# Output projections with the vector stationary and the weight rows streaming, 256 columns in each quarter of the PE array

## The chip, the cores and the metric

One core of a Trainium2 chip runs the whole program. The metric is the device time of one execution in microseconds (us); lower is better. Runs of one kernel mostly agree within about 0.15% here. The profile is of one execution; its span is about 1.8 us shorter than the device time of that execution. One profiled execution can lie away from the median of its kernel: the profile of before is of an execution of 394.29 us.

## The reference, cut to what matters

One token passes through two branches: attention over a cache of 65,536 keys (32 query heads, 4 key/value heads), and a gated MLP. A sigmoid gate mixes their outputs. The change touches only the two last matrix products, `o @ wo` and `(z1 * g) @ w_out`.

```python
def _A_ref(x, k_cache, v_cache, wq, wo):              # x 1x1x1024, caches 1x4x65536x128
    q = (x @ wq)                                       # wq 1024x4096, 32 heads of 128
    # ... softmax over 65536 keys, o: 1 x 4096
    return o @ wo                                      # wo 4096x1024
def _B_ref(x, w_in, w_sp, b_sp, w_out):
    # ... z1, g from x @ w_in: 1 x 1792 each
    return (z1 * g) @ w_out                            # w_out 1792x1024
return g * a + (1 - g) * b                             # 1 x 1 x 1024
```

Everything is bf16 with one row, so nearly all of the work is reading: 4 x 65,536 x 128 elements of K, as many of V, and about 28 MB of weights, 162 MB of loads on the page.

## The kernel before: what the change and the argument touch

Large loads go through one pool of five buffers of 32 KB a partition, all issued by SyncE in program order. The order at the end is: the last four tiles of V, `w_out` (14 chunks of 128 rows, 256 KB each), then `wo` (32 chunks), in seven pieces.

```python
WO_SPLIT = ((8, 8), (6, 4, 3, 2, 1))     # chunks of wo in each load; one buffer for each inner tuple
Q = 32                                   # columns of one quarter of the array
W = 64

def load(src, shape, name):
    t = kv.tile([P, CT * P], BF16, name=name, tag="kv")
    # [cut: a view of t in the shape asked for]
    nc.sync.dma_start(out=v, in_=src)
    return v
```

The query projection, which one experiment changes, holds a 128x128 block of weights stationary and streams one column of x, 256 times:

```python
q_ps = psm.tile([P, H], FP32, name="q_ps", tag="m")
for c in range(KC):
    w = wq_t[c // KH]
    for h in range(H):
        nc.tensor.matmul(
            q_ps[:, h:h + 1], lhsT=w[:, c % KH, h * DH:(h + 1) * DH], rhs=xT[:, c:c + 1],
            start=(c == 0 and h == 0), stop=(c == KC - 1), skip_group_check=True)
```

The output projections: eight blocks of 128x128 for a chunk, each made of every eighth column, so that partition p of the result holds eight neighbouring outputs. The vector is repeated 64 times as the moving operand.

```python
out_ps = pss.tile([P, NJ, W], FP32, name="out_ps", tag="spt")          # NJ = 8

def project(w, n, vec, c0, first=False, last=False):
    w = w.rearrange("p c (m j) -> p c j m", j=NJ)
    for c in range(n):
        for j in range(NJ):
            nc.tensor.matmul(
                out_ps[:, j, :], lhsT=w[:, c, j, :],
                rhs=vec[:, c0 + c:c0 + c + 1].to_broadcast([P, W]),
                start=(first and c == 0 and j == 0), stop=(last and c == n - 1),
                skip_group_check=True)

project(load(B_w_out.rearrange("(p c) n -> p c n", c=FC), (FC, D), "wout_t"), FC, uT, 0, first=True)
# [cut: two buffers t]
    for n in split:
        nc.sync.dma_start(out=t[:, c0 - b:c0 - b + n, :], in_=wo_view[:, c0:c0 + n, :])
        project(t[:, c0 - b:c0 - b + n, :], n, oa, c0, last=(c0 + n == OC))
        c0 += n
out_sb = const.tile([P, NJ], BF16, name="out_sb")
nc.vector.tensor_copy(out=out_sb[:], in_=out_ps[:, :, 0])
nc.sync.dma_start(out=out.rearrange("o t (p j) -> (o t p) j", j=NJ), in_=out_sb[:])
```

The value matmuls already use the streaming form: 32 stationary columns, 512 moving columns, in each of the four quarters (`o_ps[t * Q:(t + 1) * Q, :]`). In the trace of before, four of them start every 0.43 us at a granted clock of 0.50 and every 0.21 us at 1.00. They give the price of the new form.

## Time and profile before

394.06 us, median of 3 runs (393.97 to 394.17).

| | before |
|---|---|
| span of the profile | 392.5 us |
| bytes of loads, share of 16 DMA engines | 162 MB, 96.6% |
| TensorE busy | 76% |
| last matmul of the output projections ends | 389.94 us |
| cast, 128 x 8 | 0.17 us |
| output store issued, span ends | 390.16, 392.5 us |

The page of the profile before, its queues and the groups of the output projections. A queue's line gives packets, MB and the share of 16 engines' time; a group's line gives busy time, mean ns of one, and the idle time before it with what ended it:

```profile
q1 hardware_dynamic: 6480, 162.01, 96.6%
q8 instruction: 43, 0.70, 0.7%
...
L430 PE MATMUL out_ps<-oa,wo_t 128*128 128x64 bf16 x256 | 15.7, 229 | 0.6 <-DMA wo_t<-in_A_wo_dram 0.6
L430 PEld LDWEIGHTS <-wo_t 128*128 128x128 bf16 x256 | 15.6, 171 | 0.7 <-DMA wo_t<-in_A_wo_dram 0.7
...
L430 PE MATMUL out_ps<-uT,wout_t 128*128 128x64 bf16 x112 | 6.9, 235 | 3.2 <-DMA wout_t<-in_B_w_out_dram 3.2
```

DMA is the bound of the whole kernel: its queue of loads takes 96.6% of the time of the 16 engines. The projections cost 22.6 us of TensorE, and while they work on `wo` they wait 0.6 us in all.

The end of the chain of waits before, in order of time: start, duration, what.

```profile
336.97 41.19 DMA wo_t<-in_A_wo_dram
378.20 11.74 PE out_ps L430 x192
```

At 378.16 the second piece of `wo` lands, and from there 192 matmuls run without a gap to 389.94, at 61 ns each. The timeline shows the last load of `wo`, one chunk, issued by SyncE at 358.33, and the page gives 29.7 us from its issue to its landing: 388.03. So TensorE ends only 1.9 us after the last byte, and this is the most that a faster projection can give at the end.

The table by windows of the profile before: for each stretch, busy time (and instructions, those cut by an edge counted on both sides) of PE and PEld, then DVE, ACT and POOL, the granted clock, the DMA share and GB/s.

```profile
378.00:380.00 2.00, 1.80 (x30) 1.80 (x31) 0.00 (x0) 0.00 (x0) 0.00 (x0) 0.57 0.64 259
380.00:382.00 2.00, 2.00 (x37) 2.00 (x36) 0.00 (x0) 0.00 (x0) 0.00 (x0) 0.58 0.55 223
382.00:384.00 2.00, 2.00 (x37) 2.00 (x36) 0.00 (x0) 0.00 (x0) 0.00 (x0) 1.00 0.50 206
384.00:386.00 2.00, 2.00 (x37) 2.00 (x36) 0.00 (x0) 0.00 (x0) 0.00 (x0) 1.00 0.48 185
386.00:388.00 2.00, 2.00 (x37) 2.00 (x36) 0.00 (x0) 0.00 (x0) 0.00 (x0) 1.00 0.10 39
```

After 380 the DMA share is about 0.5 (0.55 to 0.48 up to 386): about half of the DMA engines have nothing left to do, while the other half needs until 386 to 388. And the pairs go at the same pace at clock 0.58 and at 1.00 (37 in 2 us), while the matmuls of the values, with 512 moving columns, take twice as long at half the clock (four in 0.43 us at 0.50, in 0.21 us at 1.00). So I take it that the moving columns do not set the 61 ns.

### The profile page before, as it was taken

The page shows a single profiled execution, that of the slowest core. Times are in us where ns is not written, and L with a number is a line of the kernel's source. Part 1 is how long each engine was busy: PE and PEld are TensorE (multiplying, and loading weights), DVE is VectorE, ACT ScalarE, POOL GpSimd, SP SyncE. Part 2 cuts the span into 40 slices and gives each one's busy share as a digit, 9 for nine tenths or more (in the row PEclk, how much of TensorE's full clock was granted, in tenths as well). Part 3 has the DMA queues.
Part 4 walks back from the last instruction along what each step waited for, and adds up shares of the span by engine and source line. Part 5 has one row for each costly group of instructions (what it writes and reads, how often), then busy time and mean ns, then how long its engine had stood idle before and what let it go on. Part 6 is the DMA issues. An engine that isn't in the chain of part 4 may idle for free.

```text
span 392.5 us, 11905 instructions
## 1 busy us (share of the span) xinstructions
PE 299.9 (76%) x5539; PEld 255.0 (65%) x5539; DVE 160.0 (41%) x316; ACT 122.2 (31%) x139; POOL 1.0 (0%) x9
## 2 busy tenths in 40 slices
PE   0774379887889985979884969689949797544697
PEld 0764379887888865857774858468738683311697
DVE  3011047574685541538551526367514357201100
ACT  1000036543594431424631423237404243100000
POOL 1000000000000000000000000000000000000000
PEclk9999999999999996999996989989978898955889
DMA  8999999999999999999999999999999999999971
GB/s 331 435 429 441 426 424 432 432 427 422 424 440 427 426 422 431 424 432 429 426 427 431 429 436 428 426 426 432 432 427 429 429 427 427 429 431 428 412 328 73
DMA packets 6566, 162.78 MB, mean 415 GB/s; under 512 B 884, under 2 KB 884, under 8 KB 1268
## 3 DMA queue, kind: packets, MB, share of 16 engines
q1 hardware_dynamic: 6480, 162.01, 96.6%
q8 instruction: 43, 0.70, 0.7%
q14 instruction: 7, 0.06, 0.0%
q10 hardware_dynamic: 36, 0.00, 0.0%
HBM read 162.01 MB, written 0.00 MB: 413 GB/s over the span
## 4 chain that ended last, share of the span: by engine, by line
DMA 50%; PE 42%; DVE 3%; issue 2%; ACT 1%; SPq 1%; DVEq 0%; ACTq 0%
DMA kn<-in_A_k_cache_dram 39%; PE tps L329 22%; DMA wo_t<-in_A_wo_dram 10%; PE spt L308 10%; PE o_ps L354 5%; PE out_ps L430 3%; DVE ktt L334 1%; DVE scT L291 1%; PE om_ps L372 1%; PE s_ps L362 1%; ACT scT L314 1%; ACT ktt L332 1%; SPq L85 0%; DVE o_sb L369 0%; PE nb_ps L286 0%
## 5 line engine op out<-in xcount | busy, mean ns | idle before, releaser
L329 PE MATMUL tps<-ident_b,kn 128*128 128x128 bf16 x2048 | 164.7, 226 | 37.3 <-DMA kn<-in_A_k_cache_dram 35.7
L329 PEld LDWEIGHTS <-kn 128*128 128x128 bf16 x2048 | 124.5, 101 | 62.8 <-DMA kn<-in_A_k_cache_dram 39.3
L334 DVE COPY ktt<-tps 128x1024 bf16<-128x1024 bf16 x171 | 116.4, 689 | 113.4 <-PE tps L329 112.6
L332 ACT COPY ktt<-tps 128x1024 bf16<-128x1024 bf16 x85 | 86.0, 1012 | 163.8 <-PE tps L329 163.8
L308 PE MATMUL spt<-qT,ktt 128*128 128x64 bf16 (+7 forms) x2048 | 104.0, 194 | 6.8 <-issue 6.7
L308 PEld LDWEIGHTS <-ktt 128*128 128x128 bf16 x2048 | 87.0, 100 | 8.4 <-issue 8.1
L354 PE MATMUL o_ps<-vt,scT 128*32 128x512 bf16 x512 | 51.9, 432 | 14.9 <-DMA vt<-in_A_v_cache_dram 14.9
L354 PEld LDWEIGHTS <-scT 128*32 128x32 bf16 x512 | 15.3, 100 | 26.7 <-issue 21.0
L314 ACT CAST scT<-spt 128x512 bf16<-128x512 f32 x32 | 18.8, 588 | 16.1 <-PE spt L308 16.1
L316 DVE TENSOR_TENSOR mxr<-scT,mxr 128x512 bf16<-128x512 bf16 x24 | 10.2, 426 | 20.3 <-ACT scT L314 18.9
L295 ACT ACTIVATE scT<-scT 128x1024 bf16<-128x1024 bf16 x16 | 16.4, 1059 | 4.9 <-DVE scT L291 4.9
L430 PE MATMUL out_ps<-oa,wo_t 128*128 128x64 bf16 x256 | 15.7, 229 | 0.6 <-DMA wo_t<-in_A_wo_dram 0.6
L430 PEld LDWEIGHTS <-wo_t 128*128 128x128 bf16 x256 | 15.6, 171 | 0.7 <-DMA wo_t<-in_A_wo_dram 0.7
L193 PE MATMUL z_ps<-xT,win_t 128*128 128x18 bf16 x224 | 13.7, 211 | 1.8 <-DMA win_t<-in_B_w_in_dram 1.3
L193 PEld LDWEIGHTS <-win_t 128*128 128x128 bf16 x224 | 13.7, 158 | 1.8 <-DMA win_t<-in_B_w_in_dram 1.4
L362 PE MATMUL s_ps<-scT,ones_b 128*32 128x512 bf16 x32 | 13.4, 418 | 0.0
L369 DVE COPY o_sb<-o_ps 128x512 f32<-128x512 f32 x4 | 2.7, 684 | 26.0 <-PE o_ps L354 26.0
L245 PE MATMUL q_ps<-xT,wq_t 128*128 128x1 bf16 x256 | 7.1, 165 | 7.6 <-DMA wq_t<-in_A_wq_dram 7.6
L245 PEld LDWEIGHTS <-wq_t 128*128 128x128 bf16 x256 | 7.0, 104 | 7.8 <-DMA wq_t<-in_A_wq_dram 7.8
L291 DVE TENSOR_TENSOR scT<-scT,negm 128x1024 bf16<-128x1024 bf16 x16 | 10.7, 683 | 0.2
L449 DVE CAST out_sb<-out_ps 128x8 bf16<-128x8 f32 x1 | 0.2, 167 | 25.1 <-PE out_ps L430 25.1
L430 PE MATMUL out_ps<-uT,wout_t 128*128 128x64 bf16 x112 | 6.9, 235 | 3.2 <-DMA wout_t<-in_B_w_out_dram 3.2
(87 smaller groups left out, 57.0 us busy)
## 6 DMA issues: line engine op xcount, KB each, us to landing
kn<-in_A_k_cache_dram SPq DMA_DIRECT2D x16, 4096.0 KB, 30.2
vt<-in_A_v_cache_dram SPq DMA_DIRECT2D x16, 4096.0 KB, 32.3
wq_t<-in_A_wq_dram SPq DMA_DIRECT2D x2, 4096.0 KB, 34.7
win_t<-in_B_w_in_dram SPq DMA_DIRECT2D x2, 3584.0 KB, 15.3
wo_t<-in_A_wo_dram SPq DMA_DIRECT2D x2, 2048.0 KB, 35.1
wout_t<-in_B_w_out_dram SPq DMA_DIRECT2D x1, 3584.0 KB
wo_t<-in_A_wo_dram SPq DMA_DIRECT2D x1, 1536.0 KB
wo_t<-in_A_wo_dram SPq DMA_DIRECT2D x1, 1024.0 KB
```

The source lines that it names most:

```text
L193: nc.tensor.matmul(z_ps[:, hf * FC + f, :], lhsT=w[:, hf, f, :], rhs=xT[:, i * KH + c:i * KH + c + 1].to_broadcast([P, zw]), start=(i == 0 ...
L245: nc.tensor.matmul(q_ps[:, h:h + 1], lhsT=w[:, c % KH, h * DH:(h + 1) * DH], rhs=xT[:, c:c + 1], start=(c == 0 and h == 0), stop=(c == KC ...
L291: nc.vector.tensor_tensor(out=blk, in0=blk, in1=negm[:].unsqueeze(1).to_broadcast([P, CT, REP]), op=ALU.add)
L295: nc.scalar.activation(out=blk, in_=blk, func=ACT.Exp, scale=SCALE)
L308: nc.tensor.matmul(spt[g][:, o:o + n], lhsT=ktt[:, j * P:(j + 1) * P], rhs=qT[:, g * REP:g * REP + n], start=True, stop=True, skip_group_c ...
L314: nc.scalar.copy(out=blk, in_=spt[g][:].rearrange("p (c h) -> p c h", h=REP))
L329: nc.tensor.transpose(tps[:, i * P:(i + 1) * P], kn[:, u * TG + i, :], ident_b[:])
L332: nc.scalar.copy(out=ktt[:], in_=tps[:])
L334: nc.vector.tensor_copy(out=ktt[:], in_=tps[:])
L354: nc.tensor.matmul(o_ps[g][t * Q:(t + 1) * Q, :], lhsT=scT[g][:, cg:cg + VC, :].rearrange("p c h -> p (c h)"), rhs=vt[:, lo:lo + VC, :].re ...
L362: nc.tensor.matmul(s_ps[g][gs, :], lhsT=ones_b[:, :Q], rhs=scT[g][:, cg:cg + CPS, :].rearrange("p c h -> p (c h)"), start=(cg == 0), stop= ...
L430: nc.tensor.matmul(out_ps[:, j, :], lhsT=w[:, c, j, :], rhs=vec[:, c0 + c:c0 + c + 1].to_broadcast([P, W]), start=(first and c == 0 and j ...
```

## The change

The intent: hold the vector stationary (one column repeated over 32 columns of the array) and stream the weight rows, 256 columns in each quarter. A chunk then takes four matmuls that should overlap as those of the values do in the trace of before (at clock 0.50 one takes up to 0.63 us, and four start every 0.43 us), each with a load of 32 stationary columns, in place of eight loads of 128 columns with eight matmuls. The result lies on four rows of 256. The split of `wo` changes too.

```diff
-WO_SPLIT = ((8, 8), (6, 4, 3, 2, 1))
+WO_SPLIT = ((16,), (8, 4, 2, 1, 1))
-    out_ps = pss.tile([P, NJ, W], FP32, name="out_ps", tag="spt")
+    NQ = P // Q
+    NO = D // NQ
+    out_ps = pss.tile([P, NO], FP32, name="out_ps", tag="spt")
     def project(w, n, vec, c0, first=False, last=False):
-        w = w.rearrange("p c (m j) -> p c j m", j=NJ)
         for c in range(n):
-            for j in range(NJ):
+            for t in range(NQ):
                 nc.tensor.matmul(
-                    out_ps[:, j, :], lhsT=w[:, c, j, :],
-                    rhs=vec[:, c0 + c:c0 + c + 1].to_broadcast([P, W]),
-                    start=(first and c == 0 and j == 0), stop=(last and c == n - 1),
+                    out_ps[t * Q:(t + 1) * Q, :],
+                    lhsT=vec[:, c0 + c:c0 + c + 1].to_broadcast([P, Q]),
+                    rhs=w[:, c, t * NO:(t + 1) * NO],
+                    start=(first and c == 0), stop=(last and c == n - 1),
                     skip_group_check=True)
-    out_sb = const.tile([P, NJ], BF16, name="out_sb")
-    nc.vector.tensor_copy(out=out_sb[:], in_=out_ps[:, :, 0])
-    nc.sync.dma_start(out=out.rearrange("o t (p j) -> (o t p) j", j=NJ), in_=out_sb[:])
+    out_sb = const.tile([P, NO], BF16, name="out_sb")
+    nc.vector.tensor_copy(out=out_sb[:], in_=out_ps[:])
+    nc.sync.dma_start(out=out.rearrange("o t (q n) -> (o t q) n", n=NO), in_=out_sb[::Q, :])
```

More of the change, by code (lines that the diff above doesn't have):

```diff
@@ L56 @@
     OC = HD // P
-    NJ = D // P
     QD = P // H
```

## The prediction

> **What bounds the kernel.** The load of the caches and weights. The page counts 162 MB on one queue, 96.6% of the span of 16 DMA engines; TensorE is busy 76%. Only the tail is open. The chain of waits ends with 41.2 us of DMA on wo_t, then 11.74 us of 192 matmuls on out_ps, unbroken from 378.20 to 389.94, then the cast (0.17 us), the output DMA (issued 390.16) and the end of the span at 392.5.
>
> **What sets those 11.74 us.** 192 LDWEIGHTS/MATMUL pairs at 61 ns, eight per 128-row chunk: 0.49 us a chunk. The last load (one chunk, 256 KB) is issued at 358.33 and lands 29.7 us later (DMA issues of the page), at 388.0. So TensorE ends only 1.9 us after the last byte. The table by windows shows why so late: after 378 the DMA share is about 0.5: half of the engines finish 8 to 10 us before the rest. The instruction queue moved 0.70 MB in 43 packets[...], and in the packet records each of these takes about 1.07 us; I read the late half as the engines that also carry them[...].
>
> **The change.** Removes 368 pairs of 128x128 weights and 64 columns; adds 184 of 128x32 weights and 256 columns, four quarters at a time. Price from the trace: the 128x512 matmuls of o_ps, which use the same quarters, go four in about 0.43 us where the granted clock is 0.50 and four in 0.21 us at 1.00; weight loads hidden. Half the columns: 0.21 us a chunk at the slow clock, 0.11 at the fast one[...]. TensorE work of the projections falls from 22.6 us to 5-10 us. But nearly all of it goes into waiting: a chunk's load costs 0.6 us, so TensorE will now wait for every piece of wo. Idle before these matmuls: 0.6 us before, about 8 to 15 us after.
>
> Bytes, buffers and order stay; wo has 6 loads, not 7. TensorE has 368 rows less, so one or two of the last instruction packets are not fetched; the one that fell at 371.8 should now come near 379.5, still on a late engine, so I leave the last landing at 387.8-388.1.
>
> **The critical path after.** Last landing 388.0; last chunk about 0.5 us with its latency (estimate from 0.376-0.634 us for one 512-column matmul): 388.5. Cast of 128x256: between 0.167 us (8 columns) and 0.684 us (512, o_sb), about 0.42: 388.95.[...] Sum: -1.9 +0.5 +0.25 -0.1 = **-1.25 us**, so 392.8 us (-0.3%). Range (8 in 10) 391.7 to 393.8. Chances: faster by over 2% 0.01, within 2% 0.98, slower 0.01.
>
> **What shows the steps right.** Out_ps matmuls busy under 11 us; the chain of waits ends in a DMA wait for wo_t, with only 4 to 8 out_ps matmuls after it; last wo_t landing at 387.5-388.3; cast 0.35-0.45 us; all before 366 us unchanged.
>
> **What would make it wrong.** If the matmuls of four quarters do not overlap at 256 columns (over 0.6 us a chunk), TensorE ends as late as before and the time is 394-396. If the missing instruction packets free the late engines, the last landing is 1.5 us earlier and the time about 391.3.[...] If the new split delays the landing, the gain vanishes.

One cut passage stood for a term of the sum: -1.9 +0.5 +0.25 -0.1 came to -1.25 us, and the -0.1 was for the output store, of whose new shape nothing had been measured; the terms that are left come to -1.15 us, or 392.9 us. The "one or two" instruction packets are an estimate from the page of before: 11,078 instructions of TensorE (5539 matmuls and 5539 weight loads) and 43 packets of the instruction queue are 258 to a packet, so 368 fewer are 1.4 packets. That the late half carries these packets, and that fewer rows would move one of them to 379.5, were estimates.

## The result, and the profile after

The changed kernel takes 392.88 us (392.74 to 393.31, 4 runs), against 394.09 us of before (393.97 to 394.17, 4 runs). The ratio is 0.9971, 95% interval 0.9954 to 0.9989: faster by 0.3%, which counts as the same at a threshold of 2%. Ratios here and below are the mean time of one kernel's runs over that of the other's of the same rounds, so not quite the ratio of the medians that are quoted.

The same lines of the page, after:

```profile
q1 hardware_dynamic: 6200, 162.01, 96.9%
q8 instruction: 42, 0.69, 0.7%
...
L430 PE MATMUL out_ps<-wo_t,oa 128*32 128x256 bf16 x128 | 7.5, 399 | 10.4 <-DMA wo_t<-in_A_wo_dram 10.4
...
L430 PEld LDWEIGHTS <-oa 128*32 128x32 bf16 x128 | 5.3, 135 | 12.8 <-issue 12.0
...
L450 DVE CAST out_sb<-out_ps 128x256 bf16<-128x256 f32 x1 | 0.4, 424 | 22.6 <-PE out_ps L430 22.6
```

The busy time on `wo` halves, 15.7 to 7.5 us, and what is saved comes back as waiting: idle before these matmuls grows from 0.6 to 10.4 us.

The end of the chain of waits after is a load; TensorE no longer has a piece in it that is worth listing:

```profile
348.63 39.01 DMA wo_t<-in_A_wo_dram
```

The timeline after, from the first piece of `wo` (start, duration, engine, line, operation, and the idle time before it). Each piece is worked off before the next one lands:

```profile
377.84 3.60 PE L430 MATMUL out_ps<-wo_t,oa 128*32 128x256 bf16 x64 [7.77 <-DMA wo_t<-in_A_wo_dram]
...
382.70 1.90 PE L430 MATMUL out_ps<-wo_t,oa 128*32 128x256 bf16 x32 [1.25 <-DMA wo_t<-in_A_wo_dram]
...
387.68 0.29 PE L430 MATMUL out_ps<-wo_t,oa 128*32 128x256 bf16 x4 [0.33 <-DMA wo_t<-in_A_wo_dram]
...
388.02 0.42 DVE L450 CAST out_sb<-out_ps 128x256 bf16<-128x256 f32 x1 [22.64 <-PE out_ps L430]
388.47 0.66 SPq L451 DMA_DIRECT2D out_dram<-out_sb  x1
```

Sixteen chunks took 3.60 us, 0.225 us a chunk, where the old form needed 0.49. Two windows of the table after:

```profile
378.00:380.00 2.00, 2.00 (x44) 1.69 (x40) 0.00 (x0) 0.00 (x0) 0.00 (x0) 0.50 0.61 258
...
384.00:386.00 2.00, 1.45 (x28) 0.90 (x21) 0.00 (x0) 0.00 (x0) 0.00 (x0) 0.50 0.44 173
```

The granted clock is 0.50 in these two windows (and 1.00 for the last three pieces, from 386.4). As each piece is worked off before the next one lands, the slow clock costs nothing here. The DMA engines are as uneven as before. The difference of the two profiles, term by term:

| term | before | after | difference, us |
|---|---|---|---|
| last landing of `wo` (completion records) | 388.06 | 387.64 | -0.42 |
| from there to the end of TensorE | 1.88 | 0.33 | -1.55 |
| cast, with the wait for it | 0.19 | 0.47 | +0.28 |
| from its end to the end of the span | 2.37 | 2.52 | +0.15 |
| span | 392.50 | 390.96 | -1.54 |

The completion records of the last piece of `wo` (sorted, us from the start of the span) show who ends last. Each load leaves 16 of them, as many as the page counts DMA engines; I read each as one engine's. The records do not name the engines.

```
before      378.31 378.34 378.55 378.87 378.96 378.96 379.69 | 382.48 | 385.89 386.00 386.25 386.30 386.35 386.39 387.85 388.06
after       377.99 378.32 378.35 378.71 378.76 378.80 379.74 | 382.32 | 385.90 385.99 386.15 386.20 386.23 386.26 386.44 387.64
```

By this reading seven engines are early, one lies between and eight are late; of these eight, two stand out by 1.5 us before, and one by 1.2 us after. The packet records give the last instruction packets (16 KB, about 1.1 us each): they start at 371.84, 379.17 and 385.79 before, and at 370.92 and 386.38 after. So before, two such packets start over 6 us before the first late engine ends (371.84 and 379.17 against 385.89), and two late engines stand out; after, one packet (370.92) and one engine. The difference of 0.42 us in the last landing is not all of that packet: over the four profiles with 42 packets (after, and experiments 1, 5 and 8) the last landing lies between 387.47 and 388.05, over the four with 43 packets (before, and experiments 2 to 4) between 387.85 and 388.07.

### The profile page after: what moved, and what is told of

Its sections match the earlier page's. It is cut to its first block, busy times and chain, and to the rows that moved or that the text cites. A ratio compares the mean times of both kernels' runs of the same rounds, so it can differ in the third digit from the quotient of the medians.

```text
span 391.0 us, 11536 instructions
## 1 busy us (share of the span) xinstructions
PE 289.8 (74%) x5355; PEld 240.1 (61%) x5355; DVE 160.2 (41%) x316; ACT 122.2 (31%) x139; POOL 1.0 (0%) x9
## 4 chain that ended last, share of the span: by engine, by line
DMA 55%; PE 39%; issue 2%; DVE 2%; ACT 1%; SPq 0%; DVEq 0%; ACTq 0%
DMA kn<-in_A_k_cache_dram 38%; PE tps L328 23%; PE spt L307 10%; DMA wo_t<-in_A_wo_dram 10%; DMA vt<-in_A_v_cache_dram 6%; PE o_ps L353 5%; DVE ktt L333 1%; ACT ktt L331 1%; PE s_ps L361 0%; PE om_ps L371 0%; SPq L84 0%; ACT scT L313 0%; DVE scT L290 0%; PE nb_ps L285 0%; PE mxT L277 0%
## 5 line engine op out<-in xcount | busy, mean ns | idle before, releaser
L353 PE MATMUL o_ps<-vt,scT 128*32 128x512 bf16 x512 | 54.2, 449 | 16.2 <-DMA vt<-in_A_v_cache_dram 15.4
L430 PE MATMUL out_ps<-wo_t,oa 128*32 128x256 bf16 x128 | 7.5, 399 | 10.4 <-DMA wo_t<-in_A_wo_dram 10.4
L192 PE MATMUL z_ps<-xT,win_t 128*128 128x18 bf16 x224 | 13.7, 208 | 1.6 <-DMA win_t<-in_B_w_in_dram 1.1
L192 PEld LDWEIGHTS <-win_t 128*128 128x128 bf16 x224 | 13.7, 158 | 1.6 <-DMA win_t<-in_B_w_in_dram 1.2
L430 PEld LDWEIGHTS <-oa 128*32 128x32 bf16 x128 | 5.3, 135 | 12.8 <-issue 12.0
L371 PE MATMUL om_ps<-o_sb,pick 128*32 128x128 f32 x32 | 5.0, 310 | 3.2 <-DVE o_sb L368 3.2
```

Source lines behind the costliest of these rows:

```text
L192: nc.tensor.matmul(z_ps[:, hf * FC + f, :], lhsT=w[:, hf, f, :], rhs=xT[:, i * KH + c:i * KH + c + 1].to_broadcast([P, zw]), start=(i == 0 ...
L353: nc.tensor.matmul(o_ps[g][t * Q:(t + 1) * Q, :], lhsT=scT[g][:, cg:cg + VC, :].rearrange("p c h -> p (c h)"), rhs=vt[:, lo:lo + VC, :].re ...
L430: nc.tensor.matmul(out_ps[t * Q:(t + 1) * Q, :], lhsT=vec[:, c0 + c:c0 + c + 1].to_broadcast([P, Q]), rhs=w[:, c, t * NO:(t + 1) * NO], st ...
```

## The experiments

Runs of the kernel before that shared the chips gave medians of 393.88 to 394.18 us.

### 1. The new form with the old split

```diff
-WO_SPLIT = ((16,), (8, 4, 2, 1, 1))
+WO_SPLIT = ((8, 8), (6, 4, 3, 2, 1))        # on the changed kernel
```

> The changed projection with the split of wo of before (8, 8, 6, 4, 3, 2, 1). Theory A (the end is set by the landing of the last piece of wo plus a fixed tail of about 0.33 us of TensorE, 0.42 us of cast and the output): the last landing is the same within 0.4 us, so the time is that of the changed kernel, 392.9 us, within 0.4. Rival B (the new split brings the gain, not the form of the matmuls): 394.0 us, as before.

Measured: 393.04 us (ratio to before 0.9977, 0.9964 to 0.9989), the last landing at 387.59 and the last matmul before 388.08. The gain is that of the whole change. The split gives nothing by itself in this form.

### 2. The old form with the new split

```diff
-WO_SPLIT = ((8, 8), (6, 4, 3, 2, 1))
+WO_SPLIT = ((16,), (8, 4, 2, 1, 1))         # on the kernel before
```

> The old projection with the new split (16, then 8, 4, 2, 1, 1). Theory A: TensorE can start on wo only when the 16-chunk piece lands, near 377.8 us, and then has 32 chunks of 0.49 us to do, so it ends near 393.5 us in place of 389.9: 397 to 398 us. Rival B (the split brings the gain): 392.9 us.

Measured: 397.87 us (1.0096, 1.0081 to 1.0112). The timeline shows 256 matmuls in one run from 377.99 to 393.56, as theory A had it:

```profile
377.99 15.57 PE L430 MATMUL out_ps<-oa,wo_t 128*128 128x64 bf16 x256 [4.14 <-DMA wo_t<-in_A_wo_dram]
```

A split that is harmless for a fast consumer costs 3.9 us with a slow one.

### 3. The old form with eleven pieces

```diff
-WO_SPLIT = ((8, 8), (6, 4, 3, 2, 1))
+WO_SPLIT = ((4, 4, 4, 4), (4, 4, 3, 2, 1, 1, 1))   # on the kernel before
```

> The old projection (128x128 weights, 64 columns, 0.49 us a chunk) with wo in eleven pieces (4, 4, 4, 4, 4, 4, 3, 2, 1, 1, 1). Theory A: a chunk's load takes about 0.62 us, longer than its 0.49 us of TensorE, so with fine pieces TensorE keeps up and ends 0.6 to 0.8 us after the last landing (1.9 us before); with the short cast (0.17 us) and the old output, 392.6 to 393.1 us: the same as the changed kernel, without the change. Rival C (the swap of operands itself is needed): 393.8 us or more.

Measured: 393.67 us (0.9993, 0.998 to 1.0005). Theory A missed here. The end of this kernel's chain of waits tells why:

```profile
331.39 35.62 DMA wout_t<-in_B_w_out_dram
367.06 22.30 PE out_ps L430 x368
```

TensorE never waits for `wo` at all: 368 pairs follow each other from the landing of `w_out`. I had priced the 32 chunks of `wo` alone (0.49 us of TensorE against 0.62 us of load), but when `w_out` lands, its 14 chunks are a backlog of 6.9 us. From that moment TensorE has 46 chunks to do, 22.3 us, while the loads still need 21.0 us (367.06 to the last landing of this run at 388.07). At 61 ns a pair the old form is bound by its throughput by about 1.3 us, whatever the split; fine pieces only recover the 0.56 us of idle time of before. The time lies between the two expectations, 0.13 us under the rival's, and is not clear of before. What the trace shows is that the projection itself has to become cheaper; that it takes the swap of operands, as the rival had it, experiment 4 does not bear out.

### 4. The old form on contiguous weights (wrong order of the result, on purpose)

```diff
-        w = w.rearrange("p c (m j) -> p c j m", j=NJ)
+        w = w.rearrange("p c (j m) -> p c j m", j=NJ)   # on the kernel of experiment 3
```

> Wrong order of the result on purpose: the old projection with eleven pieces of wo, as in the run with the fine split, but each 128x128 block of weights is 128 neighbouring columns, not every eighth. Theory I (the pair costs 61 ns because the weights are read with a step of eight elements): the pair falls to 50 to 55 ns (the score matmuls, also 64 columns on contiguous weights, take 104.0/2048 = 51 ns), the 46 chunks need about 19.5 us and TensorE waits for wo at last: it ends 0.5 to 0.9 us after the last landing, 392.9 to 393.3 us. Rival J (64 moving columns set the 61 ns): the pair stays at 61 ns, 393.7 us as with the fine split.

Measured: 393.13 us (0.9977, 0.9963 to 0.9991); TensorE ends 0.5 us after the last landing of 387.88. The groups of `wo` on the page, first of experiment 3:

```profile
L430 PE MATMUL out_ps<-oa,wo_t 128*128 128x64 bf16 x256 | 15.5, 224 | 0.0
L430 PEld LDWEIGHTS <-wo_t 128*128 128x128 bf16 x256 | 15.5, 171 | 0.0
```

and then of this run:

```profile
L430 PE MATMUL out_ps<-oa,wo_t 128*128 128x64 bf16 x256 | 12.5, 220 | 4.2 <-DMA wo_t<-in_A_wo_dram 4.2
L430 PEld LDWEIGHTS <-wo_t 128*128 128x128 bf16 x256 | 11.5, 116 | 5.1 <-DMA wo_t<-in_A_wo_dram 4.8
```

One weight load falls from 171 to 116 ns, and TensorE waits for loads again. The first 64 pairs on `wo` take 2.33 us, 36 ns each, at the full clock; at clock 0.50 32 pairs take 1.89 us, 59 ns. So the old form took 61 ns a pair because its stationary blocks were read with a step of eight elements. With contiguous blocks the pair follows the clock (36 ns at 1.00, 59 at 0.50); whether the weight load or the moving columns set its pace then, no run separates. The page of the kernel before agrees: the projection from `w_in` reads its blocks with a step of 14 elements and moves only 18 columns, and its pairs also take 61 ns (13.7 us for 224), at the full clock.

```profile
L193 PE MATMUL z_ps<-xT,win_t 128*128 128x18 bf16 x224 | 13.7, 211 | 1.8 <-DMA win_t<-in_B_w_in_dram 1.3
```

The swap of operands removes that strided weight load. Contiguous blocks would have removed most of the excess too, but then the outputs lie one by one over the partitions, and ordering them costs something that this run did not pay.

### 5. The new form with the small output (wrong result)

```diff
-    out_sb = const.tile([P, NO], BF16, name="out_sb")
-    nc.vector.tensor_copy(out=out_sb[:], in_=out_ps[:])
-    nc.sync.dma_start(out=out.rearrange("o t (q n) -> (o t q) n", n=NO), in_=out_sb[::Q, :])
+    out_sb = const.tile([P, D // P], BF16, name="out_sb")
+    nc.vector.tensor_copy(out=out_sb[:], in_=out_ps[:, :D // P])
+    nc.sync.dma_start(out=out.rearrange("o t (p j) -> (o t p) j", j=D // P), in_=out_sb[:])
```

> Wrong result on purpose: the changed kernel, but the end casts only 8 columns of 128 rows and stores 128 rows of 16 bytes, as before. Theory D (the 4-row output costs twice: 0.26 us in the cast and 0.2 to 0.3 us between issue and end, 2.53 against 2.34 us in the two traces): 392.3 to 392.5 us, 0.45 us under the changed kernel, and the span ends 2.3 us after the issue of the store. Rival (the store costs the same in both shapes): 0.26 us under the changed kernel and 2.5 us from issue to end.

Measured: 392.49 us, 0.4 us under the changed kernel. In its profile the cast takes 0.17 us and the store is issued at 388.74, with the span ending at 390.98: 2.24 us, where the changed kernel takes 2.49 (388.47 to 390.96). Its last landing happened to be at 388.05 in the profiled run, which was its slowest, 392.77; from the last landing to the end of the span it takes 2.93 us, against 3.32 in the changed kernel, again 0.4 us less. The cast gives 0.26 us of this. The store of four rows of 512 bytes costs SyncE 0.66 us of issue, against 0.35 us for 128 rows of 16 bytes: this alone is more than the store's share of the difference.

### 6. Fewer TensorE rows at the start (wrong result)

```diff
-    for c in range(KC):
+    for c in (0, 4, KC - 1):                  # q projection of the changed kernel
```

> Wrong result on purpose: the changed kernel with 160 of the 256 weight-load and matmul pairs of the q projection left out (near the start, where TensorE waits for loads anyway), 324 TensorE rows fewer. Theory E (one engine carries one instruction packet more than the other late ones, the packet at 370.9 us, and so lands the last piece 1.2 us after the third-last engine, 387.64 against 386.44 us): that packet is no longer fetched before the end, the last landing is near 386.4 us and the time 1.0 to 1.3 us under the changed kernel: 391.6 to 391.9 us. Rival (the instruction packets have nothing to do with which engine lands last): 392.9 us, last landing 387.6 us.

Measured: 391.52 us (0.9937, 0.9922 to 0.9953), 1.4 us under the changed kernel. The comparison with the reference passed it all the same, though its q is wrong. The page counts 160 matmuls and 160 weight loads fewer, so 320 rows (instructions of TensorE) and not 324 as expected. The instruction queue has 40 packets in place of 42. The last landing is 386.31, and no engine stands out any more, while the first engines end no earlier than before (378.27, and 377.99 in the changed kernel). Work that was left out between 32 and 45 us, some 345 us before the end, where TensorE waits for loads anyway (7.6 us before these matmuls), moved the last landing by 1.3 us.

### 7. A correct version of it: the streamed q

In the diff, `...` stands for `start`, `stop` and `skip_group_check`.

```diff
-    q_ps = psm.tile([P, H], FP32, name="q_ps", tag="m")
+    q_ps = [pss.tile([P, 512], FP32, name="q_ps", tag="spt") for _ in range(2)]
     for c in range(KC):
-        w = wq_t[c // KH]
-        for h in range(H):
-            nc.tensor.matmul(q_ps[:, h:h + 1], lhsT=w[:, c % KH, h * DH:(h + 1) * DH], rhs=xT[:, c:c + 1], ...)
+        for s in range(2):
+            for t in range(P // Q):
+                lo = t * (HD * Q // P) + s * 512
+                nc.tensor.matmul(q_ps[s][t * Q:(t + 1) * Q, :],
+                                 lhsT=xT[:, c:c + 1].to_broadcast([P, Q]),
+                                 rhs=wq_t[c // KH][:, c % KH, lo:lo + 512], ...)
+    q_sb = const.tile([P, REP * P], BF16, name="q_sb")
+    nc.vector.tensor_copy(out=q_sb[:, :512], in_=q_ps[0][:])
+    nc.scalar.copy(out=q_sb[:, 512:], in_=q_ps[1][:])
+    qt_ps = pst.tile([P, TG * P], BF16, name="tps")
+    for j in range(REP):
+        nc.tensor.transpose(qt_ps[:, j * P:(j + 1) * P], q_sb[:, j * P:(j + 1) * P], ident_b[:])
-    nc.vector.tensor_copy(out=qT[:, :H], in_=q_ps[:])
+    nc.vector.tensor_copy(out=qT[:, :H].rearrange("p (t j) -> p j t", j=REP),
+                          in_=qt_ps[:].rearrange("p (j t r) -> p j t r", j=REP, r=Q)[:, :, :, 0])
```

> A correct version with fewer TensorE rows: the changed kernel, with the q projection also streamed (x stationary, 512 columns of wq in each quarter, then eight 128x128 transposes): 72 pairs in place of 256, 368 rows fewer. Theory E (the number of TensorE rows sets how many instruction packets the late engines carry, and the first packet of a new round of eight costs the last landing 1.2 us): last landing near 386.4 us and the same time as with 160 pairs left out, 391.3 to 391.8 us. Rival (that run gained from the work left out at the start): 392.7 us or more.

Measured: 391.50 us (391.41 to 391.65), ratio to before 0.9937 (0.9924 to 0.9949), and correct. It beats both kernels. The projection of q itself is no faster: 7.1 us of busy time before, 7.2 us now, with 1.0 us of transposes. What it buys is rows. Over the pages, rows and packets fall together: 11,078 instructions of TensorE and 43 packets before, 10,710 and 42 in the changed kernel, 10,390 and 40 in experiment 6, 10,342 and 40 here, so 255 to 260 to a packet. Its queue of instructions, and the last lines of its timeline:

```profile
q8 instruction: 40, 0.66, 0.7%
```

```profile
386.30 0.40 PE L440 MATMUL out_ps<-wo_t,oa 128*32 128x256 bf16 x4 [0.23 <-DMA wo_t<-in_A_wo_dram]
386.75 0.42 DVE L460 CAST out_sb<-out_ps 128x256 bf16<-128x256 f32 x1 [21.32 <-PE out_ps L440]
387.20 0.65 SPq L461 DMA_DIRECT2D out_dram<-out_sb  x1
```

The completion records of its last piece:

```
streamed q  378.29 378.34 378.45 378.59 378.74 379.11 379.89 | 382.15 | 386.01 386.02 386.05 386.05 386.10 386.16 386.19 386.25
```

All eight late engines now end within 0.25 us. Forty packets would be five for each of eight engines; in the changed kernel, where the 41st starts at 370.92, well before the late engines end, one engine ends 1.2 us after the others. That the number of rows moves the last landing is shown by two runs with different edits (386.31 in experiment 6 and 386.25 here, against 387.64). That the packets go round eight engines in turn is a reading, as the records name no engines, but the completion records of earlier loads bear it out. Four of the large loads, with the packets that had started by their last completion: of the late half, as many engines end over 1 us after the others as packets are left over from whole rounds of eight, before and after the change alike:

| packets so far | 10 | 22 | 31 | 40 |
|---|---|---|---|---|
| first completion of the load, before, us | 97.55 | 184.92 | 262.60 | 350.01 |
| engines that stand out, before | 2 | 6 | 7 | 0 |
| engines that stand out, after | 2 | 6 | 7 | 0 |
| late half behind the early one, before, us | 2.1 | 4.3 | 6.0 | 7.7 |

The last line is the mean of the eight latest completions less the fourth. It is 0.2 us in the first load, before any of these packets, grows with them, and stays between 7.4 and 7.7 us from 340 to 371 us, while no packet starts between 342.72 and 371.84. So these records put the lag of the late half down to the instruction packets, at about 1.5 us for each round of eight (7.7 us after five). A packet itself takes about 1.1 us; what the rest is, and why one engine lies between the halves, stays open.

### 8. One megabyte of `wo` for half of the engines: written as 8 x 16 partitions

```diff
-WO_SPLIT = ((16,), (8, 4, 2, 1, 1))
+WO_SPLIT = ((12, 4), (8, 4, 2, 1, 1))
+            if c0 == 12:
+                nc.sync.dma_start(out=t[:, c0 - b:c0 - b + n, :],
+                    in_=A_wo.rearrange("(a e c) n -> a e c n", a=8, c=OC)[:, :, c0:c0 + n, :])
+            # [cut: else, the load as before]
```

If the early engines could carry more of the last bytes, the late ones would end earlier. Theory F is that eight engines carry this megabyte and that they are the early half; then each late one has 64 KB less to move, about 2.4 us (an estimate: four packets of 16 KB, each 614 ns in the median of the packet records of before). Rival G is that they are the late half, which then have as much more; rival H that all sixteen carry it, or some of each half. That this edit would bring it onto eight engines was the author's supposition; no run here shows it, and the reasons given are cut, here and in experiments 9 and 11.

> The changed kernel with the 16-chunk piece of wo split into 12 chunks and 4 chunks, and the 4 chunks (1 MB) loaded with the DRAM side written as 8 x 16 partitions.[...] Theory F[...]: the last landing moves from 387.6 to about 385.2 us and the time falls to 390.3 to 391 us. Rival G[...]: the last landing moves to about 390 us, time 395.3 us. Rival H[...]: within 0.4 us of 392.9, or in between.

Measured: 392.96 us, against 392.88 of the changed kernel, and the piece left 16 completion records like any other, so rival H. Nothing is learned about which engines are early.

### 9 and 10. The same megabyte as sixteen loads of 8 partitions

Experiment 9 is on the changed kernel, 10 on the one with the streamed q.

```diff
+            if c0 == 12:
+                for i in range(0, P, 8):
+                    nc.scalar.dma_start(out=t[i:i + 8, c0 - b:c0 - b + n, :],
+                                        in_=wo_view[i:i + 8, c0:c0 + n, :])
+            # [cut: WO_SPLIT as in 8; else, the load as before]
```

> The changed kernel with 4 of the first 16 chunks of wo (1 MB) loaded as 16 loads of 8 partitions each, issued by ScalarE.[...] Theory F[...]: last landing near 385.2 us, time 390.3 to 391 us. Rival G[...]: last landing near 390 us, time 395.3 us. Rival H (mixed): in between, or as the changed kernel. Whatever the engines, if the sixteen loads come too late, TensorE's wait for them shows in the timeline before chunk 12.

> Both together. If theories E and F hold, the gains add, up to the engine that lies between the two halves (382.3 us in the changed kernel): last landing near 384.5 us, time 389.3 to 390.2 us. If G holds: 394 us.

Measured: 407.30 and 407.05 us. The timeline of the first one shows SyncE issuing its last four pieces of `wo` over 37.5 us from 353.34, and ScalarE twelve of its loads over 42 us from 353.14, and TensorE waiting 12.04 us before chunk 12. In the trace the loads share eight completion semaphores. ScalarE's load at 373.33, for one, follows the landing, at 373.3, of the load that used its semaphore before, and SyncE waits 49.9 us in all for landings of `wo`. The loads came too late, so neither F nor G is tested.

### 11 and 12. Fewer loads of odd width

On the kernel with the streamed q, the 16-chunk piece in five loads, all from SyncE, and then, as a control, in two. Theories F to H are those of experiment 8, for the four loads of 8 partitions. Theory K is that the load of 96 partitions slows the packets even without loads of 8.

```diff
+            cuts = [0, P] if c0 else [0, 96, 104, 112, 120, P]      # 11: four_small_pieces
+            cuts = [0, P] if c0 else [0, 96, P]                     # 12: two_part_piece
+            for lo, hi in zip(cuts, cuts[1:]):
+                nc.sync.dma_start(out=t[lo:hi, c0 - b:c0 - b + n, :],
+                                  in_=wo_view[lo:hi, c0:c0 + n, :])
```

> The version with the streamed q, with the 16-chunk piece of wo loaded as 96 partitions and then four loads of 8 partitions (1 MB), all from SyncE, so that only four extra loads queue and none comes late.[...] Theory F[...]: last landing 384 to 385 us in place of 386.3, time 389.3 to 390.5 us in place of 391.5. Rival G[...]: last landing near 388.7 us, time 393.9 us. Rival H (mixed): in between, or 391.5 us.

> The version with the streamed q, with the 16-chunk piece of wo loaded as 96 partitions and 32 partitions[...]. Theory K (in the run with four small pieces the packets slowed[...]): the 32 KB packets again take 2 us or more and the time is 400 us or more. Rival L (the four loads of 8 partitions alone did it): 391.3 to 392 us, packets 1.2 us.

Measured: 420.71 and 410.16 us, slower by 29 and 19 us than the kernel with the streamed q. Windows of that kernel:

```profile
350.00:360.00 10.00, 4.74 (x42) 1.68 (x38) 0.00 (x0) 0.00 (x0) 0.00 (x0) 0.67 1.01 435
360.00:370.00 10.00, 6.90 (x86) 4.04 (x79) 2.83 (x8) 0.00 (x0) 0.00 (x0) 0.67 1.00 426
```

and of the run with 96 and 32 partitions:

```profile
350.00:360.00 10.00, 4.75 (x42) 1.70 (x38) 0.00 (x0) 0.00 (x0) 0.00 (x0) 0.50 1.03 396
360.00:370.00 10.00, 2.92 (x30) 1.40 (x23) 2.73 (x8) 0.00 (x0) 0.00 (x0) 0.84 1.02 211
370.00:380.00 10.00, 3.18 (x56) 2.33 (x55) 0.00 (x0) 0.00 (x0) 0.00 (x0) 0.50 1.01 189
```

The DMA engines are as busy as ever (share 1.0) and move half as much. In the packet records the median 32 KB packet takes 1.22 us up to 357, and 2.52 us from 358 to 365; packets of `w_out`, itself a normal load of 128 partitions, slow down beside them from 1.07 to 2.22 us. Theory K's numbers came true: splitting the load into 96 and 32 partitions is enough, without any load of 8. Why such loads slow the others was not tested, and which engines are the early ones stays open as well, since in every run that steered the bytes something else decided.

## Why the prediction was right, point by point

The predicted time was 392.8 us and the measured one 392.88. The sum held, though one term had the wrong sign and one event was misplaced, and these two partly cancelled. That it held to 0.1 us is luck: the terms of the table add up to -1.54 us, the medians differ by 1.21 us, and -1.25 was forecast.

- **"TensorE ends only 1.9 us after the last byte"**: this sized the gain. 11.7 us of TensorE work could be made cheaper, but only what reached past the last landing could be won. The profile after shows 0.33 us there, where 0.5 was estimated, and 10.4 us of waiting in place of 0.6 ("about 8 to 15"). Experiments 1 and 3 confirm it from two sides: the new form reaches the landing with either split, and the old form does not reach it even with eleven pieces. Experiment 4 adds that an old form made cheaper comes to within 0.5 us of it too: what counts is the price of the projection, of which the swap is one remedy.
- **The price of the new form**, 0.21 us a chunk at the slow clock, read from the 512-column value matmuls: 0.225 measured. The loads of 32 stationary columns show no cost in the trace after: 64 matmuls took 3.60 us, and 3.30 us of weight loads lay beside them.
- **The cast**, about 0.42 us between two known sizes: 0.424.
- **The output store**, -0.1 us in the sum, with no measurement behind it: wrong in sign. It became 0.15 us longer, of which experiment 5 gives the cause: the shape of the store, with SyncE's issue of 0.66 against 0.35 us.
- **The instruction packets.** That the late half carries them held: experiments 6 and 7 move the last landing to 386.3 by removing rows, and the table of experiment 7 shows the lag growing with the packets. The prediction had named that case as one that would make it wrong, at about 391.3 us; it did not arise because the change removed one packet, 43 to 42, and it takes 40 to free the late engines (391.50 us in experiment 7). But "the one that fell at 371.8 should now come near 379.5" did not: it came at 370.92, while TensorE was waiting for the first piece of `wo` (idle for 7.77 us up to 377.84). Why it came no later with fewer rows was not tested. One late engine stood out all the same, as said. The last landing came 0.42 us earlier in the profile, where the sum had put zero; as the other profiles scatter by as much, part of this may be chance.

## What to carry to other kernels

When a kernel is bound by loads, price a faster consumer by the time between the last landing and the consumer's end, not by its busy time; and count the backlog that it has when the last stream begins, or a finer split will look like a cure. Look at the spread of the completions of a wide load: here the last one came up to 9.7 us after the first (377.99 to 387.64 in the changed kernel). The rows of the TensorE program are loads too (43 packets and 0.70 MB before), and fewer of them can move the end even when they are left out some 345 us before it: 320 rows fewer moved the last landing from 387.64 to 386.31. They did it in steps: here what counted was to get from 42 packets to 40, a multiple of eight. Do not balance engines by loading fewer partitions at a time without measuring, since here this halved the rate of the loads in flight, from 426 to 211 GB/s.
